# A planned kernel of attention, a state-space convolution and a gate: Toeplitz loads spaced by waits on score sets, another model of instruction supply, and a new rank for the last convolution

## The chip, the cores and the metric

The kernel runs on one core of one Trainium2 chip. The metric is the device time of one execution in microseconds (us); the median of several runs is compared. The engines of the core run side by side, each with its own queue of instructions, executed in order: TensorE (PE), VectorE (DVE), ScalarE (ACT), GpSimd (POOL) and SyncE (SP). They wait for each other by semaphores. Transfers are started by SP, POOL and ACT and carried out by the core's DMA engines.

## The reference

One sequence of 2048 tokens, width 448. Three results are mixed: attention `a` with 16 query heads of width 28 and one shared key and value head, a diagonal state-space layer `b` (256 complex states per channel) computed as a long convolution, and a gate `g`.

```python
x = A_x
g = _sigmoid((x * gate_w).sum(-1, keepdims=True))
# attention: q from x @ wq (16 heads), k = x @ wk, v = x @ wv
scores = jnp.einsum("bhqd,bkd->bhqk", q, k) * (Dh ** -0.5)
p = _softmax(scores, axis=-1)
o = jnp.einsum("bhqk,bkd->bhqd", p, v)
a = o.transpose(...).reshape(B, S, H * Dh) @ wo
# state-space layer: a kernel K per channel, then a causal convolution of length 2048
P = jnp.exp(logdA[:, :, None] * l[None, None, :])
K = jnp.einsum("dn,dnl,dn->dl", Cc, P, dB).real
y = irfft(rfft(u) * rfft(K))[:L]
b = y + u * Dskip
return g * a + (1 - g) * b
```

## The kernel before

Two streams of work run side by side.

**Attention.** The scores are cut into 1024 tiles of 128 keys by 512 queries. They are taken in sets of three and two tiles by turns, 410 sets in all; a set fills three or two of five PSUM banks. For each set PE computes the scores (L1318 with four heads in row groups, L1341 with full rows; L1329 and L1332 at the end), and ACT takes one exponential over the whole set (L1373) into the tile `expT`. PE then multiplies with the values (L1392, L1386 at the end) into bank 6. Query projections (`qproj`, L873 and L882), norms and output projections (`outp`, L1133) come once per block of 64 tiles.

**Convolution.** The 448 channels are worked in 14 groups `c` of 32. For each, DVE builds tables of powers (`tables`, L954 to L1004), PE multiplies them into the kernel K (`kgen`, L1027), DVE copies it to `kstg` (L1039), and POOL writes it to the DRAM scratch `KP`. From there SP loads Toeplitz matrices (`tload`): 56 loads, each of four `dma_start` calls with 1024 rows of 1088 bytes, into three buffers in the tile `T`, from load 42 on also into two in `U`. A convolution (`conv`, 28 of them, 16 channels each) reads two loads: 128 small matmuls (L1094) into one PSUM bank, a gated copy to `cst` on DVE (L1104), 64 transposing matmuls by pieces of 16 (L1115), and an addition into the output tile `O` (L1124). `ufill` copies inputs from `T` to `U` by SP for convolutions 14 and later.

Banks 5 and 7 are shared by `conv`, `kgen`, `qproj` and `outp`: an operation with a `lock` takes one of them at its first matmul, and the one with `unlock` gives it back.

**The end.** After the last exponential the last half block is normed (`scaled`, L1197 to L1210) and projected (`last`, L1231); L1237 adds what is in `O`. One store goes out from ACT's queue and the others from SP's.

**The order.** The order on every engine is fixed before the program runs, by a planner (`Prog.schedule`). It walks through time with an estimated cost for each operation, and at each step takes the operation that can start first, ties broken by the rank `pr` (a lower one goes first). `self.waits` then turns the dependencies `o.deps` into waits on semaphores, so a dependency added while planning becomes a real wait. Terms used below:

- A load's slot is `T0` to `T4`, so `o.slot[0] == "T"` picks the Toeplitz loads.
- `block` models how PE's instructions arrive: blocks of 256 (`BLOCK`) after a first 158 (`FIRST`). When the planned PE instructions pass the end of a block, the next one is planned to be there `FETCH` (4800 ns) later, and `IDLE` (3300 ns) from 480 us on. An operation with a rank of 1 or more also leaves a reserve (`NEED`).
- `LAZY` gives operations of ranks 1.15, 1.55, 1.58 and 1.6 a margin of 200 ns after what they wait for, and 1000 ns after a Toeplitz load before 300 us (`LATE`).
- Where PE would be idle too long, the planner puts in a filler matmul (L1300).

Of the kernel before, what the change touches and what calls it, by code (L numbers as in the profile page):

```python
# [61 lines left out]
class Buf:  # L62
    def __init__(self, handle):
        self.h = handle
        self.rs = handle[:].ap[0][0]
# [26 lines left out]
class Prog:  # L92
# [4 lines left out]
    SAME = {"act": 100.0, "dve": 125.0, "pool": 150.0}  # L97
    SWITCH = 105.0
    BLOCK, FIRST, FETCH, IDLE, NEED, QUIET = 256, 158, 4800.0, 3300.0, 0.015, 480000.0
    HALF = (0.0, 0.0, 1.0)  # L100
    PORT = 0.55
    POOL = (7, 5)
    SLACK = {"pe": 500.0, "dve": 300.0}
# [5 lines left out]
    def __init__(self, nc, es):  # L109
        self.nc, self.es = nc, es  # L110
        self.ops = []
        self.lastw = {}
        self.readers = {}
        self.slots = {}
        self.commops = {}
        self.after = {}
        self.filler = None

    def op(self, eng, fn, ns, rd=(), wr=(), pr=0, lat=None, lock=None, unlock=None, comm=None, mode="f", ni=0):
        o = Op()  # L120
# [59 lines left out]
    def schedule(self):  # L180
        ops = self.ops
# [17 lines left out]
        order = {e: [] for e in ENG}  # L199
        locks = [[None, 0.0, [], b] for b in self.POOL]  # L200
        mode = None
# [3 lines left out]
        npe = 0  # L205
        block = [0.0, 0.0]
        opened = False
        past = []
        self.tot = {}
        self.clock = {e: {} for e in ENG}  # L210
# [4 lines left out]
        while done < n:  # L215
            best = None
            for e in ENG:
                T = free[e]
                for i in ready[e]:
                    o = ops[i]  # L220
                    r = max(rt[i], T)
                    if o.lock is not None:
                        L = min((x for x in locks if x[0] is None), key=lambda x: x[1], default=None)
                        if L is None:
                            continue
                        r = max(r, L[1] + (300.0 if o.pr >= 2 else 0.0))
                    for k in o.comm or ():
                        if k in comm:
                            r = max(r, ops[comm[k]].end)
                    if e == "pe":  # L230
                        j = (npe + o.ni - self.FIRST - 1) // self.BLOCK + 1
                        if j < len(block):
                            r = max(r, block[j])
                            if o.pr >= 1 and block[-1] > r:
                                left = self.FIRST + (len(block) - 2) * self.BLOCK - npe - o.ni
                                r = max(r, block[-1] - left / self.NEED)
                    key = (r, o.pr, i)
                    if best is None or key < best[0]:
                        best = (key, e, i)
            assert best is not None, "scheduler stuck"  # L240
            (r, _, _), e, i = best
            o = ops[i]
            spare = [x for x in locks if x[0] is None and x[1] <= free[e]]
            if e == "pe" and (opened or spare) and r > self.FWIN and self.filler is not None and npe > self.FIRST + self.BLOCK:
                T = free[e]
                j = (npe + 2 - self.FIRST - 1) // self.BLOCK + 1
                w = self.FILL + (self.SWITCH if mode != "f" else 0.0) + (self.SWITCH if o.mode != "f" else 0.0) - 50.0
                past = [x for x in past if x[1] > T - self.FWIN]
                busy = sum(x[1] - max(x[0], T - self.FWIN) for x in past)
                if r - T >= w and busy < self.FLOW * self.FWIN and (j >= len(block) or block[j] <= T):  # L250
                    b = 6 if opened else spare[0][3]
                    o = self.op("pe", lambda x, b=b: self.filler(x, b), self.FILL, rd=["one", "id"], ni=2)
                    if not opened:
                        for d in spare[0][2]:
                            o.deps[d] = 1
                    rt.append(0.0)
                    need.append(0)
                    succ.append([])
                    n += 1
                    i, r = o.i, T  # L260
                    ready[e].append(i)
            ready[e].remove(i)
            if e == "pe" and o.mode != mode:
                r = max(r, free[e] + self.SWITCH)
                mode = o.mode
            if e == "pe":
                past.append((r, r + o.ns * o.act))
                opened = o.psb == 1 if o.psb else opened
            if e == "pool" and o.slot is None:
                for d in reversed(order[e]):  # L270
                    if ops[d].slot is None:
                        o.deps[d] = 1
                        break
            order[e].append(i)
            for k in o.comm or ():
                if k in comm:
                    o.deps[comm[k]] = 1
                comm[k] = i
            if o.lock is not None:
                L = min((x for x in locks if x[0] is None), key=lambda x: x[1])  # L280
                for d in L[2]:
                    o.deps.setdefault(d, 1)
                L[0] = o.lock
                o.lock.bank = L[3]
                L[2] = []
            nw = self.waits(e, o)
            if e == "pe":
                npe += o.ni + max(0, nw - 1)
                while npe > self.FIRST + (len(block) - 2) * self.BLOCK:
                    block.append(r + (self.FETCH if r < self.QUIET else self.IDLE))  # L290
            if o.slot is not None:
                free[e] = r + o.iss * o.ndma
                s = r if e == "pool" else max(r, dmafree)
                end = max(s + o.ns, free[e]) + self.DMA_NS + o.extra
                dmafree = max(dmafree, s) + o.ns
            else:
                ns = o.ns
                if e == "pe" and self.HALF[0] < r < self.HALF[1]:
                    ns *= self.HALF[2]
                free[e] = r + ns  # L300
                end = free[e] + o.lat
                if e == "pool" and o.ns >= 500.0:
                    free["dve"] = max(free["dve"], r) + self.PORT * o.ns
            o.end = end
            if o.unlock is not None:
                L = [x for x in locks if x[0] is o.unlock][0]
                L[0], L[1] = None, end + self.SEM_NS
                L[2].append(i)
            for j in succ[i]:
                need[j] -= 1  # L310
                x = ops[j]
                if i not in x.deps:
                    t = free[e]
                elif x.eng == e and o.slot is None and e == "pe":
                    t = free[e]
                elif x.eng == e and o.slot is None:
                    t = free[e] + self.SAME[e]
                else:
                    t = end + self.SEM_NS
                    if x.eng == "pe" and x.pr in self.LAZY:  # L320
                        t += self.LAZY[x.pr] if o.slot is None else self.LATE if o.slot[0] == "T" and r < 300000.0 else 0.0
                    if x.pr == 1.45:
                        t += self.FAR
                    elif x.pr >= 2 or x.pr == 1.5:
                        t += self.SLACK.get(x.eng, 0.0)
                rt[j] = max(rt[j], t)
                if need[j] == 0:
                    ready[x.eng].append(j)
            done += 1
# [79 lines left out]
class Kernel:  # L409
# [669 lines left out]
    def conv(self, c):  # L1079
        pg = self.pg  # L1080
        X = ("cx", c)
        cs = c % 2
        ps = px = self.grp()
        for k in range(4):
# [5 lines left out]
            for n in range(8):  # L1090
                def mm(e, k=k, n=n, to=to, gi=gi, tbuf=tbuf):
                    m0, par = 2 * (n // 2), n % 2
                    for j in range(4):
# [4 lines left out]
                    return r  # L1098
                first = k == 0 and n == 0
                o = pg.op("pe", mm, 56, mode="c", ni=8, rd=[("T", s), ("Uc", c % 14), ("Ub", 0), ("Ub", 1)] + [("Uf", c % 14, j) for j in range(7)],  # L1100
                      wr=[X] + ([("cst", cs)] if first else []), pr=1.6,
                      lock=ps if first else None)
                self.cm[c, 8 * k + n] = o.i
        pg.op("dve", lambda e: e.tensor_tensor(self.cst.v(0, P, cs * 512, [[128, 4], [64, 2], [1, 64]]),  # L1104
# [3 lines left out]
        Y = ("yx", c)  # L1108
# [9 lines left out]
                                 start=(mu == 0), stop=(mu == 1), tile_position=(0, 64 * par), skip_group_check=True)  # L1118
            return r
        for k in range(4):  # L1120
            o = pg.op("pe", lambda e, k=k: yt(e, k), 70, mode="h", ni=8, rd=[("cst", cs), "id"], wr=[Y], pr=1.55)
        self.lastC = o.i
        ov = self.O.v(0, P, 15 * D + 16 * c, [[-D, 16], [1, 16]])
        pg.op("dve", lambda e: e.tensor_tensor(ov, ov, px.v(0, P, 0, [[1, 16], [16, 16]]), ALU.add),  # L1124
# [363 lines left out]
```

## Time and profile before

| | us |
|---|---|
| median of 3 runs | 500.31 (500.03 to 502.58) |
| the profiled execution's own time | 499.53 |
| its span, first to last instruction | 497.8 |
| first exponential L1373 starts | 21.30 |
| last exponential ends | 490.73 |
| last table operation on DVE (L1004) ends | 453.52 |
| Toeplitz loads issued | 80.74 to 473.92 |

How to read it: the span is the stretch that the profile shows, and the time of the execution contains 1.73 us around it. In a row of a timeline the first number is the start, the second the length, then engine, line, operation, output and input, and how many instructions were merged into the row; in brackets stands the idle time of the engine just before it and what ended that. SPq is SP's queue of transfers: the length there is the time of issuing, not of moving data. "issue" names idle time in which the engine waited for no semaphore that the profile shows. A row of a table by stretches gives the stretch, its length, busy time of the engine and the number of instructions, the granted TensorE clock, the share of DMA and GB/s. A group's row gives the busy time, the mean of one in ns, and the idle time ahead of the group with what ended most of it.

### The profile page before, as it was taken

The numbers are of one execution on the slowest core, as the hardware profiler recorded it, in microseconds if no ns is written. First come the engines' busy times: TensorE is split into PE (matmuls) and PEld (weight loads), VectorE is DVE, ScalarE is ACT, GpSimd is POOL, SyncE is SP. The second block draws the span as 40 slices with busy tenths as digits, with TensorE's granted clock in tenths as the row PEclk, the third lists the DMA queues.
The fourth block names the chain that finished last, engine by engine and source line by source line (L and its number), as shares of the span: only waits on it lengthen the run. The fifth ranks groups of instructions, "written<-read, shape, count | busy, mean of one in ns | idle before, by whom it ended". The sixth has DMA issues, their size and how long they took to land.

```text
span 497.8 us, 17345 instructions
## 1 busy us (share of the span) xinstructions
PE 476.5 (96%) x7641; PEld 208.2 (42%) x7641; DVE 455.1 (91%) x867; ACT 484.2 (97%) x436; POOL 146.2 (29%) x282
## 2 busy tenths in 40 slices
PE   8899999999999999899999999999999999999997
PEld 6432233343443444444344344444444344344553
DVE  6999999999999999999999999998999999995313
ACT  6999999999999999999999999999999999999995
POOL 2102044234143433224306044520612524251110
PEclk9999999999999999999999999999999999999999
DMA  8997696928529556893953962689793596759742
GB/s 266 324 173 185 118 157 133 261 74 250 152 49 284 166 155 126 247 246 57 288 129 51 285 156 77 184 244 290 176 283 39 144 314 185 212 135 302 234 160 70
DMA packets 152423, 91.86 MB, mean 185 GB/s; under 512 B 84538, under 2 KB 148332, under 8 KB 152348
## 3 DMA queue, kind: packets, MB, share of 16 engines
q1 hardware_dynamic: 143370, 81.21, 61.4%
q0 software_dynamic: 8704, 9.41, 7.6%
q8 instruction: 60, 0.98, 0.8%
q10 hardware_dynamic: 274, 0.14, 0.1%
q14 instruction: 15, 0.12, 0.1%
HBM read 73.61 MB, written 5.23 MB: 158 GB/s over the span
## 4 chain that ended last, share of the span: by engine, by line
ACT 86%; PE 7%; DMA 2%; issue 0%; SPq 0%
ACT expT L1373 85%; DMA T<-KP_scratch 2%; PE psS L1341 1%; PE psS L1318 1%; PE psB L1392 1%; PE psB L1294 1%; PE psS L1231 1%; PE psX L1094 0%; PE psS L1094 0%; SPq L158 0%; PE psB L1300 0%; PE psS L1027 0%; PE psS L873 0%; PE psB L1386 0%; PE psX L1027 0%
## 5 line engine op out<-in xcount | busy, mean ns | idle before, releaser
L1373 ACT ACTIVATE expT<-psS 128x1536 bf16<-128x1536 f32 (+1 forms) x410 | 464.5, 1410 | 2.5 <-PE psS L1341 1.5
L968 DVE TENSOR_TENSOR tab<-tab,mbf 128x512 bf16<-128x512 bf16 (+4 forms) x140 | 139.7, 1002 | 0.0
L1318 PE MATMUL psS<-qT,kT 29*128 29x512 bf16 x684 | 95.7, 385 | 10.7 <-ACT expT L1373 5.5
L1392 PE MATMUL psB<-expT,vaug 128*32 128x512 bf16 x1000 | 99.9, 390 | 0.1
L1341 PE MATMUL psS<-qM,kT 128*128 128x512 bf16 x316 | 95.1, 384 | 1.2 <-ACT expT L1373 0.5
L158 POOL DMA_DIRECT2D KP_scratch<-kstg x104 | 57.4, 559 | 78.1 <-DVE kstg L1039 74.8
L983 DVE TENSOR_TENSOR tab<-tab 128x256 bf16<-128x256 bf16 (+4 forms) x140 | 77.3, 576 | 0.0
L1392 PEld LDWEIGHTS psB<-expT,vaug 128*32 128x32 bf16 x1000 | 25.6, 93 | 73.3 <-issue 70.5
L158 POOL DMA_DIRECT2D qM<-qT x64 | 32.4, 514 | 62.9 <-DVE qT L885 33.0
L1318 PEld LDWEIGHTS psS<-qT,kT 29*128 29x128 bf16 x684 | 23.7, 91 | 64.3 <-ACT expT L1373 51.8
L1300 PE MATMUL psB<-ident,one 128*128 128x512 bf16 x148 | 48.2, 384 | 0.0
L158 POOL DMA_DIRECT2D rdenB<-R_scratch x60 | 31.0, 523 | 48.8 <-DMA R_scratch<-denT 48.7
L1094 PE MATMUL psX<-T,U 128*26 128x128 bf16 (+3 forms) x1728 | 38.6, 221 | 1.2 <-issue 1.0
L1094 PE MATMUL psS<-T,U 128*26 128x128 bf16 (+3 forms) x1536 | 35.6, 221 | 1.1 <-DMA T<-KP_scratch 1.1
L1094 PEld LDWEIGHTS psX<-T,U 128*26 128x26 bf16 (+3 forms) x1728 | 29.6, 105 | 15.0 <-issue 10.0
L158 POOL DMA_DIRECT2D denT<-acc x15 | 10.7, 711 | 85.6 <-DVE acc L1153 72.6
L1094 PEld LDWEIGHTS psS<-T,U 128*26 128x26 bf16 (+3 forms) x1536 | 27.3, 105 | 13.3 <-issue 7.6
L997 DVE TENSOR_TENSOR tab<-tab,tmp 128x1984 bf16<-128x1984 bf16 x28 | 32.4, 1184 | 0.0
L1341 PEld LDWEIGHTS psS<-qM,kT 128*128 128x128 bf16 x316 | 19.0, 97 | 28.5 <-ACT expT L1373 19.5
L991 DVE TENSOR_TENSOR tmp<-tmp,mq 128x64 bf16<-128x64 bf16 (+4 forms) x70 | 25.4, 363 | 0.0
L914 DVE TENSOR_TENSOR msq<-seedz 128x512 f32<-128x512 f32 (+1 forms) x40 | 24.7, 618 | 0.0
L1300 PEld LDWEIGHTS psB<-ident,one 128*128 128x128 bf16 x148 | 13.3, 97 | 22.1 <-issue 14.4
(186 smaller groups left out, 491.2 us busy)
## 6 DMA issues: line engine op xcount, KB each, us to landing
T<-KP_scratch SPq DMA_DIRECT2D x204, 272.0 KB, 4.9
U<-KP_scratch SPq DMA_DIRECT2D x20, 272.0 KB, 5.5
rdenB<-R_scratch POOLq DMA_DIRECT2D x60, 64.0 KB, 4.1
U<-cst SPq DMA_DIRECT2D x1, 3584.0 KB, 25.0
qM<-qT POOLq DMA_DIRECT2D x64, 32.0 KB, 3.3
tab<-in_A_x_dram SPq DMA_DIRECT2D x4, 448.0 KB, 4.7
O<-in_A_x_dram SPq DMA_DIRECT2D x16, 112.0 KB, 4.8
O<-cst SPq DMA_DIRECT2D x1, 1792.0 KB, 9.6
```

The lines of the kernel that those rows point to most:

```text
L158: return [e.dma_start(o, i, **kw) for o, i in pairs]
L914: pg.op("dve", lambda e: e.tensor_tensor(m2(msq), z2, z2, ALU.mult), el(2 * n), rd=[kr, ki] + first, wr=["msq"], pr=pr)
L968: mul = lambda e, o, a, b: e.tensor_tensor(o, a, b, ALU.mult)
L983: vo(lambda e, dv=dv, tv=tv, k=k: e.tensor_tensor(dv, dv, tv, ALU.add if k else ALU.subtract), n, [kt[k], kd[k]], [kd[k]], 1.92 if lv else ...
L991: vo(lambda e, w=w, lv=lv: e.tensor_tensor(rho.v(0, P, (32 - 2 * w) * 2, [[64, 32], [2, w], [1, 2]]), rho.v(0, P, (32 - w) * 2, [[64, 32], ...
L997: vo(lambda e, k=k: e.tensor_tensor(tab.v(0, P, FM + k * FP + 2, [[64, 32], [2, 31], [1, 2]]), tab.v(0, P, lm + k * PL + 62, [[64, 32], [- ...
L1094: r = e.matmul(ps.v(32 * j, 32 - m0, 128 * k, [[1, 128]]), self.U.v(0, P, (4 * gi + j) % UA // 2 * 128 + 2 * (2 * m0 + par) + j % 2, [[4, ...
L1300: return e.matmul(t.v(0, P, off, [[1, 512]]), self.one.v(0, P, 2, [[0, P]]), self.ident.v(0, P, 0, [[0, 4], [1, P]]), start=b != 6, stop=b ...
L1318: r = e.matmul(self.psS.v(0, P, 512 * b, [[1, 512]]), kT.v(32 * h, DH + 1, 128 * kt, [[1, 128]]), qT.v(32 * h, DH + 1, 512 * (i % 2), [[1, ...
L1341: return e.matmul(self.psS.v(0, P, 512 * b, [[1, 512]]), kT.v(0, P, 128 * kt, [[1, 128]]), self.qM.v(0, P, (i % 2) * XQ + 512 * h, [[1, 51 ...
L1373: o = pg.op("act", lambda e: e.activation(expT.v(0, P, 512 * es[0], spread(es, n)), self.psS.v(0, P, 512 * bs[0], spread(bs, n)), AF.Exp, ...
L1392: r = e.matmul(self.psB.v(32 * h, 32, 0, [[1, 512]]), vaug.v(0, P, 32 * kt, [[1, 32]]), expT.v(0, P, 512 * ring[t], [[1, 512]]), start=(kt ...
```

## The change

Three things are altered in the planner and in two ranks; no operation of the computation is added or taken away.

```diff
     BLOCK, FIRST, FETCH, IDLE, NEED, QUIET = 256, 158, 4800.0, 3300.0, 0.015, 480000.0
+    LOAD, BEHIND, ALONE, BEGUN = 2600.0, 3700.0, 700.0, 300.0
+    OPEN = (80000.0, 440000.0)
+    GAP, SPACED = 6500.0, (80000.0, 440000.0)
...
+        self.moving = []
...
+        lastT = 0.0
...
+                    if o.slot is not None and o.slot[0] == "T" and self.SPACED[0] < r < self.SPACED[1]:
+                        r = max(r, lastT + self.GAP)
                     key = (r, o.pr, i)
...
+            if o.slot is not None and o.slot[0] == "T":
+                if self.SPACED[0] < r < self.SPACED[1]:
+                    for d in reversed(order["act"]):
+                        if ops[d].end <= r:
+                            o.deps[d] = 1
+                            break
+                lastT = r
...
                 while npe > self.FIRST + (len(block) - 2) * self.BLOCK:
-                    block.append(r + (self.FETCH if r < self.QUIET else self.IDLE))
+                    behind = max((z - r for b, z in self.moving if b < r - self.BEGUN), default=0.0)
+                    block.append(r + (self.LOAD + min(max(behind, self.ALONE), self.BEHIND) if self.OPEN[0] < r < self.OPEN[1]
+                                      else self.FETCH if r < self.QUIET else self.IDLE))
...
+                if o.ns > 1000.0 and e == "sp":
+                    self.moving = [x for x in self.moving if x[1] > r - 20000.0] + [(r, end)]
...
-                      wr=[X] + ([("cst", cs)] if first else []), pr=1.6,
+                      wr=[X] + ([("cst", cs)] if first else []), pr=1.6 if c < 27 else 0.85,
...
-            o = pg.op("pe", lambda e, k=k: yt(e, k), 70, mode="h", ni=8, rd=[("cst", cs), "id"], wr=[Y], pr=1.55)
+            o = pg.op("pe", lambda e, k=k: yt(e, k), 70, mode="h", ni=8, rd=[("cst", cs), "id"], wr=[Y], pr=1.55 if c < 27 else 0.8)
```

Between 80 and 440 us of planned time a Toeplitz load is planned no sooner than 6.5 us after the one before, and it gets a wait for the last operation on ACT that the plan has ended by then, which is mostly the exponential of a score set. In the same stretch a block of PE instructions is planned to arrive 3300 ns after the one before when nothing is moving, and up to 6300 ns when a transfer of SP (a Toeplitz load or the larger of the U copies) began at least 300 ns earlier and is still under way, by what is left of it. The matmuls of convolution 27 get the rank 0.85 instead of 1.6 and its transposes 0.8 instead of 1.55; with that they no longer fall under `LAZY` and leave no reserve of instructions.

## The prediction

> **What bounds the kernel now.** I read the page's shares first, then its chain of waits, then the timelines of the two places where that chain leaves ScalarE.
>
> ```profile
> PE 476.5 (96%) x7641; PEld 208.2 (42%) x7641; DVE 455.1 (91%) x867; ACT 484.2 (97%) x436; POOL 146.2 (29%) x282
> ...
> q8 instruction: 60, 0.98, 0.8%
> ...
> ACT 86%; PE 7%; DMA 2%; issue 0%; SPq 0%
> ...
> L1373 ACT ACTIVATE expT<-psS 128x1536 bf16<-128x1536 f32 (+1 forms) x410 | 464.5, 1410 | 2.5 <-PE psS L1341 1.5
> ```
>
> ScalarE is busy for 97% of the span, and 410 exponentials (L1373) are 464.5 of its 484.2 us. The idle column gives only 2.5 us ahead of them. It understates a little, since neighbours overlap, so I took the starts from the trace: the next exponential begins 1.330 us (median) after one of three tiles and 0.903 us after one of two. What exceeds these medians sums to 6.26 us between 80 and 440 us, and that is all the change can win in the stretch it re-plans. Two places hold 2.86 us of it. First, by the timeline at 208 us:
>
> ```profile
> 208.13 0.41 PE L1094 MATMUL psX<-T,U 128*26 128x128 bf16 x15
> 209.51 0.49 PE L1094 MATMUL psX<-T,U 128*30 128x128 bf16 x21 [0.96 <-issue]
> ...
> 210.58 1.02 ACT L1373 ACTIVATE expT<-psS 128x1024 bf16<-128x1024 f32 x1 [0.56 <-PE psS L1341]
> ...
> 211.80 1.45 ACT L1373 ACTIVATE expT<-psS 128x1536 bf16<-128x1536 f32 x1 [0.20 <-PE psS L1318]
> ```
>
> PE stops for 0.96 us in a run of equal matmuls with no semaphore to wait for. Queue q8 moved 60 blocks (0.98 MB, 16 KB each); 7641 matmuls, as many weight loads and 61 waits are 15,343 instructions, so a block holds 256. In the DMA records the block asked for near 203.05 moved only at 207.03 to 208.18, when the load issued at 200.84 was ending (its data to 207.48). From 80 to 440 us, request to arrival took 1.6 to 3.2 us where no load was moving, and up to 5.8 us behind one that had just begun. The two late exponentials lost 0.90 and 0.32: 1.22 us. Second, at 339 us:
>
> ```profile
> 338.14 0.40 PE L1392 MATMUL psB<-expT,vaug 128*32 128x512 bf16 x4
> ...
> 339.60 0.25 PE L1094 MATMUL psS<-T,U 128*32 128x128 bf16 x4 [1.06 <-DMA T<-KP_scratch]
> ...
> 340.74 2.60 ACT L1373 ACTIVATE expT<-psS 128x1024 bf16<-128x1024 f32 x2 [0.75 <-PE psS L1341]
> ```
>
> A convolution matmul stands in PE's queue before its Toeplitz load has landed, and the scores behind it are late. Here 0.88 and 0.25 are lost, and at 329.2 and 336.3 us, after like waits, 0.20 and 0.33: 1.64 us. The other 3.40 us are some twenty pieces of 0.05 to 0.27 us, behind long runs of convolution, table or projection matmuls between two score sets.
>
> SyncE's queue, by its timeline, shows how the loads come:
>
> ```profile
> 196.24 16.36 SPq L158 DMA_DIRECT2D T<-KP_scratch  x16
> 213.16 0.71 SPq L158 DMA_DIRECT2D U<-T  x1
> 214.28 5.16 SPq L158 DMA_DIRECT2D T<-KP_scratch  x4
> 219.48 15.90 SPq L158 DMA_DIRECT2D U<-T  x7
> 235.43 4.83 SPq L158 DMA_DIRECT2D T<-KP_scratch  x6
> ```
>
> Four issues are one load: five loads within 23 us, then 16 us of none. Between 80 and 440 us, 31 of 47 gaps between load starts are under 6.5 us, the least 2.6; alone, a load's data move for 3.1 to 4.6 us.
>
> VectorE is the second bound:
>
> ```profile
> 80.00:440.00 360.00, 355.57 (x663) 1.00 0.67 181
> ```
>
> It idles 4.43 us in 360 (busy 355.57), 1.14 and 1.28 of that in the same two stalls.
>
> **The change, part by part.** *Spacing of loads.* Enforcing 6.5 us on the trace's starts pushes a load by 4.6 us on average, by 12.9 at most; every group but one is caught up before the next comes. A block request then meets at most one load, and a load no other's data, so its landing is what the plan assumes. I take 1.4 of the 1.64 us as gained: the 0.20 at 329.2 came from a landing only 0.26 us late, without a margin of its own past 300 us. Bounds: 0 and 1.64.
>
> *The wait itself.* It adds no instruction to ScalarE. SyncE stands on the score set; behind it are later loads, the U copies and the early stores. A U copy is first needed by convolution 14 (it starts at 281.43 in the trace), while the copies begin at 185.2, so tens of us of cover exist. Without it a late copy would cost what the late loads cost, 0.2 to 1.1 us each. Price: 0.
>
> *The supply model.* A block was planned 4.8 us after the one before; now 3.3 with nothing moving and up to 6.3 behind a load. Both lie above what the trace shows for their case (3.2, 5.8), so the 1.22 us should go; I take 1.2, bounds 0 and 1.22.
>
> [...]
>
> *What the new plan costs.* 3.3 instead of 4.8 lets PE's runs be 1.45 times as dense between loads, and loads moved by 4.6 us of a table cycle of 29.4 us (kgen's last copies, L1039, at 77.3 and 459.0, over 13 cycles) put 16% of the convolution work into stretches that now hold other work. No row shows such a plan. From the 3.40 us of small pieces: 16% is 0.5, 45% is 1.5; I take 0.9, toward the lower, since the loads' bursts are also thinned. Bounds: all small pieces gone (3.4 gained), or doubled (3.4 lost).
>
> *Convolution 27.* Its 128 matmuls and 4 groups of transposes pass the output projections (rank 0.9) in PE's queue, lose the 0.2 us margin after a load, and ignore the reserve on instruction blocks. Its two loads keep their rank, and the stores that its sum releases (SyncE, 488.26) end before ScalarE issues the last one at 495.57, so they gain nothing. The rows at the end:
>
> ```profile
> 485.57 0.69 DVE L1104 TENSOR_TENSOR cst<-psS,omq 128x512 bf16<-128x512 f32 x1 [4.90 <-PE psS L1094]
> ...
> 487.81 0.42 DVE L1124 TENSOR_TENSOR O<-O,psS 128x256 bf16<-128x256 bf16 x1 [0.68 <-PE psS L1115]
> ...
> 492.19 0.35 PE L1237 MATMUL psS<-O,ident 128*128 128x448 bf16 x1
> ...
> 495.00 0.54 ACT L1254 ACTIVATE O<-psS 128x448 bf16<-128x448 f32 x1 [1.89 <-PE psS L1231]
> ```
>
> The last row is also the end of the chain of waits. Convolution 27 ends VectorE's 4.90 us wait at 485.57; its sum is done at 488.23, and PE reads O again at 492.19. Earlier by 2 to 3 us, it frees PE from other work before 490.73, where the last exponential ends. The 7.07 us after that are the last half's own path, with at most 0.4 us of queueing: onT ends at 493.98, the last projection starts at 494.61. I take 0.2; bounds 0.4 gained to 0.3 lost, if a block of instructions (one is crossed at 490.78) moves into this path.
>
> *Sum:* -1.2 - 1.4 + 0.9 - 0.2 = -1.9 us. Bounds: -1.22 - 1.64 - 3.4 - 0.4 = -6.7 and 3.4 + 0.3 = +3.7. The profiled execution took 499.53 (span 497.8 and 1.73 around it), so it becomes 497.6. The median of the runs is 0.78 above it, at 500.31 (500.03 to 502.58), and becomes **498.4**. A difference of 0.5%, 2.5 us, is about what can be told here from no change.
>
> **Rivals.** *The stalls move.* The order of some 15,000 instructions is made anew; one new stall of the size seen (1.22, or 1.13 from the set at 340) and small pieces at their upper estimate (1.5) leave -1.2 - 1.4 + 1.5 + 1.1 - 0.2 = -0.2: 500.1. For it: ScalarE has no more than two score sets of cover, so any PE stop of 1 us shows. The wait ties SyncE to a score set and not to a time, so a load that is late for another reason still pushes its successor. Against: the places that set off the two stalls are what the new model describes. Chance 0.25, of which 0.04 is that a block's delay doesn't depend on loads at all. That mechanism would keep the 1.22: -1.4 + 0.9 - 0.2 = -0.7, 499.6. The block that waited from 203.05 to 207.03 speaks against it. [...]
>
> *Thinner all round.* Spread loads break up the long convolution runs and the small pieces halve: -1.2 - 1.6 - 1.7 + 0.5 = -4.0, 496.3, where 0.5 is what remains of new lateness. For it: convolutions follow landings in groups now. Against: it needs all parts to pay. Chance 0.17.
>
> *Slower: PSUM held longer.* A convolution takes one of two banks (5 and 7) from its first matmul to its last sum, 12.0 us on average, and needs two loads. With starts 6.5 apart instead of about 3.3 it holds 3.2 us more: 30.4 instead of 24.0 of each cycle's 58.7 bank-us. Table matmuls (kgen), query projections and output projections use the same two; a late kgen holds up VectorE's next tables, and VectorE has no slack to 440 us. At the end there are 3.96 us of cover, 488.23 to 492.19, so it decides from 0.28 us per cycle (3.96/14). At 0.5 us per cycle VectorE ends 7.0 later: 7.0 - 4.0 = +3.0, 503.3. For it: 355.57 of 360 busy. Against: 28 bank-us per cycle are left for the others, and query projections have a 29 us period. Chance 0.20.
>
> **How the numbers follow.** The forecast itself has 0.38, with its own range 497.2 to 499.8. The range 496.0 to 502.6 takes in the second and third cases and part of the fourth. Faster by over 0.5% (under 497.8): 0.17 and about a third of 0.38, 0.30. Slower (over 502.8): 0.20. Within: 0.50.
>
> **What would show it.** The 0.96 us stop on "issue" and the 1.06 us wait for T are gone, exponentials' idle time is under 2.5 us, no two load starts between 80 and 440 us are under 6 us apart, VectorE's wait ahead of the last L1104 is under 4 us. If "issue" stops of half a microsecond appear between loads, 3.3 was too little; if VectorE idles clearly over 4.43 us before 440 us with kgen's copies (L1039) waiting, the slower rival is right. An idle gain at unchanged time would mean that the exponentials themselves became slower.

## The result, and the profile after

The changed kernel takes 503.06 us (median of 20 runs, 500.51 to 505.75) against 500.29 for the one before (20 runs, 498.74 to 505.63): a ratio of 1.0049, interval 1.003 to 1.0068. (Ratios here and below compare fast runs alone and are not the ratio of the two medians.) It became slower by 2.8 us where 1.9 of gain were forecast, and lies above the forecast's range of 496.0 to 502.6. By each run's mean granted clock (one stretch of 3.4 us at half the clock, as the profile of after shows two, takes 3.4 * 0.5/500 = 0.003 off it), 16 of the 20 runs of after had one or two such stretches and 25 of 106 of the kernel before had any; the runs of the kernel before with one are about 2.6 us longer (medians 502.4 and 499.8), and the 4 of after without one have a median of 501.4. The profiled execution of after took 504.81 (span 503.1), 1.75 above the median, and has two of these stretches (0.993), so its losses are larger than those of a typical run. Rows of its page:

```profile
PE 464.9 (92%) x7555; PEld 209.1 (42%) x7639; DVE 455.6 (91%) x867; ACT 484.5 (96%) x436; POOL 145.3 (29%) x282
...
ACT 71%; DVE 12%; PE 11%; DMA 3%; SPq 2%; issue 1%; POOL 0%
...
L1391 ACT ACTIVATE expT<-psS 128x1536 bf16<-128x1536 f32 (+1 forms) x410 | 464.7, 1403 | 6.7 <-PE psS L1336 4.2
```

This trace has 7555 matmuls beside 7639 weight loads (7641 of each before): 84 records of matmuls are missing, so PE's busy time is understated here, and weight loads are the better count. The exponentials themselves cost what they did (464.7 us against 464.5); their idle time rose from 2.5 to 6.7, and ScalarE's share of the chain of waits fell from 86 to 71%. Counted as in the prediction (starts beyond 1.330 and 0.903 us after the one before), lateness from 80 to 440 us hardly moved, 6.26 before and 6.40 after. Past 440 us, which the change does not re-plan, it rose from 0.65 to 4.77, and the tail after the last exponential grew from 7.06 to 7.79. Of the profiled execution's 5.3 us of loss, 4.1 and 0.7 lie there.

**Inside the stretch.** Both stalls shown of before are gone: at 208 us PE runs without a stop, and no 1.06 us wait stands at 339. A new place took over, by the timeline at 234 us:

```profile
233.89 0.48 PE L1112 MATMUL psX<-T,U 128*32 128x128 bf16 x20 [1.06 <-DMA T<-KP_scratch]
...
234.74 1.45 ACT L1391 ACTIVATE expT<-psS 128x1536 bf16<-128x1536 f32 x1 [0.79 <-PE psS L1336]
...
236.00 0.63 PE L1359 MATMUL psS<-qM,kT 128*128 128x512 bf16 x1 [0.33 <-issue]
...
236.68 1.02 ACT L1391 ACTIVATE expT<-psS 128x1024 bf16<-128x1024 f32 x1 [0.49 <-PE psS L1359]
...
238.39 1.45 ACT L1391 ACTIVATE expT<-psS 128x1536 bf16<-128x1536 f32 x1 [0.69 <-PE psS L1336]
```

A convolution waits 1.06 us for load 18, and three sets in a row are late, by 1.05, 0.61 and 0.81 us: 2.47 together, nearly the 2.86 that the two old stalls held. Only the first is the wait itself. The table by stretches (columns: the stretch and its length, then busy time of PE, its weight loads, DVE, ACT, POOL, then clock, DMA share, GB/s) has the rest:

```profile
232.00:235.20 3.20, 2.14 (x58) 1.25 (x60) 3.20 (x10) 2.41 (x3) 1.42 (x3) 0.93 0.67 119
235.20:238.40 3.20, 2.87 (x53) 1.27 (x43) 3.20 (x9) 2.02 (x3) 0.00 (x0) 0.53 1.01 293
238.40:242.00 3.60, 3.50 (x21) 1.10 (x20) 3.60 (x8) 3.60 (x4) 0.57 (x1) 1.00 0.72 158
```

After the wait the granted TensorE clock is about half, 0.53 in this row: the record of the clock has 0.5 from 234.78 us on for 3.41 us. One 512-column matmul, 0.38 to 0.39 us elsewhere, lasts 0.63 there.

**Past 440 us.** Before, ScalarE's row there is one unbroken run of 46 exponentials; after, it is broken:

```profile
438.84 51.89 ACT L1373 ACTIVATE expT<-psS 128x1536 bf16<-128x1536 f32 x46
```

```profile
439.38 16.08 ACT L1391 ACTIVATE expT<-psS 128x1536 bf16<-128x1536 f32 x14
456.20 22.74 ACT L1391 ACTIVATE expT<-psS 128x1536 bf16<-128x1536 f32 x20 [0.75 <-PE psS L1336]
480.70 1.45 ACT L1391 ACTIVATE expT<-psS 128x1536 bf16<-128x1536 f32 x1 [1.76 <-PE psS L1336]
482.74 1.02 ACT L1391 ACTIVATE expT<-psS 128x1024 bf16<-128x1024 f32 x1 [0.59 <-PE psS L1359]
484.25 11.02 ACT L1391 ACTIVATE expT<-psS 128x1536 bf16<-128x1536 f32 x10 [0.49 <-PE psS L1347]
```

PE's rows of after at the two breaks name what stopped the scores:

```profile
455.52 0.32 PE L1133 MATMUL psS<-ident,cst 128*64 128x60 bf16 x7 [1.00 <-issue]
...
479.64 0.70 PE L1112 MATMUL psX<-T,U 128*26 128x128 bf16 x36 [2.00 <-issue]
```

These are stops in runs of equal matmuls with no semaphore to wait for, the kind that stood at 208 us before. By the planner's count a block is asked for when PE has issued 158 + 256 j instructions (weight loads, matmuls and waits). The trace has no record of the request, so this moment is an estimate; in the profiles of before and after each of the 60 records on queue q8 begins behind one such point, 0.6 us at the soonest, and its end is the arrival. In all profiles of this case together, PE has 20 stops of over 0.6 us on "issue" after 80 us, and each lies 35 or 36 instructions behind such a point. At the one of before and the two of after, PE goes on 1.24 to 1.57 us after a block's arrival (at 208.18, 453.95 and 478.40). So they are taken here for stops at the border of a block. The block asked for at 470.76 arrived at 478.40, 7.6 us later; the blocks asked for at 448.14 and 453.78 took 5.8 and 7.2, and before, blocks behind loads in this stretch took 3.4 to 5.3. SyncE's queue after shows what they stood behind:

```profile
438.74 2.55 SPq L162 DMA_DIRECT2D T<-KP_scratch  x4
...
443.38 5.69 SPq L162 DMA_DIRECT2D T<-KP_scratch  x8
449.12 5.96 SPq L162 DMA_DIRECT2D U<-KP_scratch  x8
...
466.23 8.18 SPq L162 DMA_DIRECT2D T<-KP_scratch  x12
474.45 2.64 SPq L162 DMA_DIRECT2D U<-KP_scratch  x4
```

The last eight loads come back to back in both kernels, 2.6 to 3.9 us apart within each group of four (before they start at 440.19 to 450.52 and at 462.18 to 470.49): the spacing ends at 440 us. What differs is the work that meets them. Counting weight loads, as many matmuls, and waits, PE has 2542 instructions left at 440 us after and 2399 before. Of the 143 more, 72 convolution matmuls with their weight loads make 144, and the rest cancels. Before's stretch there, by the table by stretches, had PE busy for 48.26 of 50 us and ScalarE without a gap (columns: PE, weight loads, DVE, ACT, POOL, clock, DMA share, GB/s):

```profile
440.00:490.00 50.00, 48.26 (x1164) 25.09 (x1160) 22.17 (x34) 50.00 (x46) 7.78 (x15) 1.00 0.68 208
```

### The profile page after: what moved, and what is told of

It reads as the page before. It is cut to its first block, busy times and chain, and to the rows that moved or that the text cites. A ratio compares the mean times of both kernels' runs of the same rounds, so it can differ in the third digit from the quotient of the medians.

```text
span 503.1 us, 17277 instructions
## 1 busy us (share of the span) xinstructions
PE 464.9 (92%) x7555; PEld 209.1 (42%) x7639; DVE 455.6 (91%) x867; ACT 484.5 (96%) x436; POOL 145.3 (29%) x282
## 4 chain that ended last, share of the span: by engine, by line
ACT 71%; DVE 12%; PE 11%; DMA 3%; SPq 2%; issue 1%; POOL 0%
ACT expT L1391 71%; DVE tab L986 3%; DVE tab L1001 2%; PE psS L1359 2%; DMA qM<-qT 2%; SPq L162 2%; PE psB L1410 1%; PE psS L1336 1%; DMA T<-KP_scratch 1%; PE psX L1112 1%; DVE tab L1015 1%; PE psS L656 1%; PE psB L1318 1%; DVE tmp L1009 1%; PE psS L1249 1%
## 5 line engine op out<-in xcount | busy, mean ns | idle before, releaser
L1391 ACT ACTIVATE expT<-psS 128x1536 bf16<-128x1536 f32 (+1 forms) x410 | 464.7, 1403 | 6.7 <-PE psS L1336 4.2
L1359 PE MATMUL psS<-qM,kT 128*128 128x512 bf16 x243 | 79.2, 384 | 12.6 <-issue 8.8
L1112 PE MATMUL psX<-T,U 128*26 128x128 bf16 (+3 forms) x1728 | 40.2, 225 | 3.1 <-issue 2.0
L1112 PEld LDWEIGHTS psX<-T,U 128*26 128x26 bf16 (+3 forms) x1728 | 30.8, 107 | 18.9 <-issue 13.0
L1015 DVE TENSOR_TENSOR tab<-tab,tmp 128x1984 bf16<-128x1984 bf16 x28 | 32.2, 1182 | 0.1
L1318 PEld LDWEIGHTS psB<-ident,one 128*128 128x128 bf16 x145 | 12.9, 97 | 21.7 <-issue 14.9
```

The costliest lines, as they stand in the source:

```text
L1015: vo(lambda e, k=k: e.tensor_tensor(tab.v(0, P, FM + k * FP + 2, [[64, 32], [2, 31], [1, 2]]), tab.v(0, P, lm + k * PL + 62, [[64, 32], [- ...
L1112: r = e.matmul(ps.v(32 * j, 32 - m0, 128 * k, [[1, 128]]), self.U.v(0, P, (4 * gi + j) % UA // 2 * 128 + 2 * (2 * m0 + par) + j % 2, [[4, ...
L1318: return e.matmul(t.v(0, P, off, [[1, 512]]), self.one.v(0, P, 2, [[0, P]]), self.ident.v(0, P, 0, [[0, 4], [1, P]]), start=b != 6, stop=b ...
L1359: return e.matmul(self.psS.v(0, P, 512 * b, [[1, 512]]), kT.v(0, P, 128 * kt, [[1, 128]]), self.qM.v(0, P, (i % 2) * XQ + 512 * h, [[1, 51 ...
L1391: o = pg.op("act", lambda e: e.activation(expT.v(0, P, 512 * es[0], spread(es, n)), self.psS.v(0, P, 512 * bs[0], spread(bs, n)), AF.Exp, ...
```

## The experiments

Three theories were set against each other. A: the change pushes convolution work past 440 us, where loads come back to back and blocks are planned at a flat time, and the loss is made there. B: any new order has new stalls, wherever they fall. C: the prediction's slow rival, PSUM banks held longer.

**One part at a time.** Each of the first three keeps one part of the change and puts the others back.

```diff
-    OPEN = (80000.0, 440000.0)
+    OPEN = (0.0, 0.0)
...
-                      wr=[X] + ([("cst", cs)] if first else []), pr=1.6 if c < 27 else 0.85,
+                      wr=[X] + ([("cst", cs)] if first else []), pr=1.6,
...
-            o = pg.op("pe", lambda e, k=k: yt(e, k), 70, mode="h", ni=8, rd=[("cst", cs), "id"], wr=[Y], pr=1.55 if c < 27 else 0.8)
+            o = pg.op("pe", lambda e, k=k: yt(e, k), 70, mode="h", ni=8, rd=[("cst", cs), "id"], wr=[Y], pr=1.55)
```

> Only the spacing of the loads and its waits; supply model and last rank as before. Theory A (work pushed past 440 us meets an end in which loads come back to back and blocks of instructions are planned at a flat 4.8 us): slower than before by most of the change's loss, ratio 1.003 to 1.008, with stops on issue of 1 to 2 us after 440 us. Theory B (any new order has one or two stalls of its own, wherever they fall): anything from 0.997 to 1.008, stalls not tied to the end. Theory C (convolutions hold PSUM longer, VectorE late): ratio as in A, but VectorE's idle time before 440 us over 8 us, against 4.4 before the change.

Measured: 503.88 against 500.26, 1.0082 (1.0053 to 1.0111). 2545 instructions were left at 440 us.

```diff
-    GAP, SPACED = 6500.0, (80000.0, 440000.0)
+    GAP, SPACED = 6500.0, (0.0, 0.0)
...
-                      wr=[X] + ([("cst", cs)] if first else []), pr=1.6 if c < 27 else 0.85,
+                      wr=[X] + ([("cst", cs)] if first else []), pr=1.6,
...
-            o = pg.op("pe", lambda e, k=k: yt(e, k), 70, mode="h", ni=8, rd=[("cst", cs), "id"], wr=[Y], pr=1.55 if c < 27 else 0.8)
+            o = pg.op("pe", lambda e, k=k: yt(e, k), 70, mode="h", ni=8, rd=[("cst", cs), "id"], wr=[Y], pr=1.55)
```

> Only the supply model between 80 and 440 us; no spacing, rank as before. Theory A: the stop near 208 us is gone and nothing is pushed past 440, so 1.2 us faster to equal: ratio 0.996 to 1.001. Theory B: anything from 0.997 to 1.008. Theory C: not slower, ratio 0.997 to 1.001.

Measured: 504.31, 1.0088 (1.0057 to 1.0119); 2490 instructions left.

```diff
-    OPEN = (80000.0, 440000.0)
+    OPEN = (0.0, 0.0)
...
-    GAP, SPACED = 6500.0, (80000.0, 440000.0)
+    GAP, SPACED = 6500.0, (0.0, 0.0)
```

> Only the two ranks of convolution 27. All theories: the order differs only in the last 25 us or so; ratio 0.998 to 1.002. If the ranks alone cost more than 1 us, a part of the loss is that the last convolution takes PE's time from the last score sets.

Measured: 500.30, 1.0001 (0.9979 to 1.0023). Each of the first two parts alone costs over 0.8%, more than the whole change (the intervals overlap), and the rank alone nothing. In the profiles of the first two the lateness of 80 to 440 us is 6.53 and 6.07, near the 6.26 of before, so B's stalls do not add up there; VectorE idles 4.75 and 4.43 us in that stretch, where C asked for more than 8. Past 440 the lateness is 2.02 and 2.40, and the tail 9.99 and 9.98 instead of 7.06.

A, too, was right only in part. It had the time of the first run, but not its stops of 1 to 2 us: past 440 us PE's longest stop on "issue" there is 0.5 us, and most of the loss is the tail. It missed the second (0.996 to 1.001 expected), since the supply model alone also leaves work behind at 440 us. And the third profile, in which PE's order is that of before up to 478 us, has a block that took 7.0 us (asked for at 450.95) and a stop of 1.10 us at 452.94 us, where before's profile has none: one profile does not tell how often an order stops.

**Is it the transfers at the end?** The changed kernel in its own order, with the last eight loads cut to a fraction of their bytes:

```diff
-            to = bass.AP(tensor=buf.h, offset=h * rs + o, ap=[[4 * rs, 32], [TC, 8], [1, TC]])
+            n = TC if gi < 48 else 32
+            to = bass.AP(tensor=buf.h, offset=h * rs + o, ap=[[4 * rs, 32], [TC, 8], [1, n]])
-            lst.append((to, dram(self.KP, h * 512 + 1 + 8 * gi * KW, [[1, 32], [KW, 8], [1, TC]])))
+            lst.append((to, dram(self.KP, h * 512 + 1 + 8 * gi * KW, [[1, 32], [KW, 8], [1, n]])))
```

> The changed kernel in the same order, with loads 48 to 55 moving 32 of each row's 544 elements; the rest of these rows keeps older data, so part of the convolution of the last channels is left out. Theory A: blocks asked for after 440 us come within 3 us, the stops of 1.0 and 2.0 us on issue are gone, the last exponential ends near 491, ratio 0.997 to 1.001. Theory B agrees if its stalls are supply stalls. Theory C: PSUM and order are unchanged, so the loss stays, ratio 1.003 to 1.007.

Measured: 499.93 against 500.26, 0.999 (0.9964 to 1.0017). ScalarE's timeline from 440 us on is whole again:

```profile
439.61 51.82 ACT L1392 ACTIVATE expT<-psS 128x1536 bf16<-128x1536 f32 x46
```

Blocks asked for past 440 us took 1.7 to 3.8 us there. The table by stretches, the changed kernel first, this one second (columns as above):

```profile
440.00:490.00 50.00, 44.15 (x1095) 23.50 (x1103) 21.50 (x32) 46.41 (x41) 9.18 (x17) 0.97 0.74 227
```

```profile
440.00:490.00 50.00, 48.11 (x1192) 25.46 (x1195) 22.63 (x35) 50.00 (x45) 8.89 (x18) 1.00 0.30 60
```

In the same order PE issues 1195 weight loads in the 50 us instead of 1103. So PE can do the larger backlog in time, and what went with the bytes of the loads are the stops on "issue". Whether the thinner loads land sooner themselves was not shown; the stops that went were not on T. How much is lost beside full loads depends on where the blocks and stops fall: e1_spacing_only and g1_spacing_supply_capped, whose orders leave as much work, issue 1172 and 1182 weight loads in these 50 us with the same 227 GB/s moving and at full clock. The same thin loads in the kernel before are the control:

> The control for the thinned loads: the kernel before in its own order, loads 48 to 55 moving 32 of 544 elements (a part of the last channels' convolution is left out). Theory A: before has no backlog and only 0.65 us of lateness after 440 us, so little to regain: 0.997 to 1.000. If thinning speeds up any order by what the changed kernel regained: 0.993 to 0.996, and the thinned runs prove nothing about the backlog.

Measured: 500.47 against 499.79, 1.0004 (0.998 to 1.0029). The thin loads are worth nothing where the backlog is 682 matmuls (as counted just below) and the whole loss where it is 752.

**Is it the backlog?** The kernel before, where only convolution 22 may not begin before score set 370 (it began at 437.3 us). Measured by what the planned order leaves after the 960th value matmul, 713 matmuls of all kinds are then left, against 682 before and 752 in the change. In the traces 436, 404 and 476 of those left are matmuls of convolutions, which is the whole difference:

```diff
+            if s == HOLDSET:
+                self.holdset = o.i
...
+        pg.after[self.cm[22, 0]] = self.holdset
```

> The kernel before, with one thing altered: convolution 22 may not begin before score set 370 (near 445 us; in the kernel before it begins at 437.5). Up to there the order is the one of before, after it about 50 more matmuls are left than before, as in the changed kernel. Theory A (backlog at the end, where blocks of instructions wait behind back-to-back loads): slower by about the change's loss or more, since the last rank is as before: ratio 1.003 to 1.010, stops on issue after 450 us, and convolution 27 ends 5 to 10 us later than 485.5. Theory B (stalls fall where they like): 0.998 to 1.003. Theory C (PSUM held longer, VectorE late before 440 us): no change, 0.999 to 1.002.

Measured: 502.36 against 500.18, 1.0029 (1.0003 to 1.0055). This is just under A's range and inside B's, and convolution 27 ends 4.0 us later than before, not 5 to 10, so time alone does not decide between the two. The same marks as in the change appear in its profile, PE first, then ScalarE:

```profile
478.26 0.86 PE L1095 MATMUL psX<-T,U 128*28 128x128 bf16 x48 [0.80 <-issue]
```

```profile
439.24 39.66 ACT L1376 ACTIVATE expT<-psS 128x1024 bf16<-128x1024 f32 x35
479.50 4.63 ACT L1376 ACTIVATE expT<-psS 128x1536 bf16<-128x1536 f32 x4 [0.60 <-PE psS L1319]
484.67 8.72 ACT L1376 ACTIVATE expT<-psS 128x1536 bf16<-128x1536 f32 x8 [0.54 <-PE psS L1330]
```

With the thin loads on top:

> As the run with convolution 22 held, in the same order, and loads 48 to 55 move 32 of each row's 544 elements (a part of the last channels' convolution is left out). Theory A: the blocks come within 3 us, the loss is gone, ratio 0.997 to 1.001. If instead the late convolutions themselves are the cost, whatever the blocks do, the loss stays: 1.003 to 1.010.

Measured: 501.03, 1.0002 (0.998 to 1.0024). None of the change's three parts is in these kernels. Holding back one convolution makes a small loss, and with thin loads none can be told. The two intervals overlap, so that the loss goes with the transfers rests here on the profiles: lateness past 440 us is 2.13 us with full loads and 0.59 with thin ones, 0.65 before. The loss is smaller than the change's; how much of the rest is the larger backlog, the place at 234 us and the clock was not separated.

**The rank in company.** The change without it:

```diff
-                      wr=[X] + ([("cst", cs)] if first else []), pr=1.6 if c < 27 else 0.85,
+                      wr=[X] + ([("cst", cs)] if first else []), pr=1.6,
...
-            o = pg.op("pe", lambda e, k=k: yt(e, k), 70, mode="h", ni=8, rd=[("cst", cs), "id"], wr=[Y], pr=1.55 if c < 27 else 0.8)
+            o = pg.op("pe", lambda e, k=k: yt(e, k), 70, mode="h", ni=8, rd=[("cst", cs), "id"], wr=[Y], pr=1.55)
```

> The changed kernel with convolution 27 ranked as before. Theory A: the rank is what saves the end in the changed kernel, whose stretch after the last exponential was 7.8 us against 10.0 in the two runs of one part alone: ratio 1.007 to 1.012, and that stretch is 9.5 to 10.5 us. If the rank does nothing: 1.004 to 1.006.

Measured: 504.68 against 500.18, 1.0095 (1.0063 to 1.0127), beside 1.0049 (1.003 to 1.0068) with it. Its timeline of ScalarE at the end:

```profile
483.22 8.72 ACT L1391 ACTIVATE expT<-psS 128x1536 bf16<-128x1536 f32 x8 [1.15 <-PE psS L1347]
497.22 0.98 ACT L1272 ACTIVATE O<-psS 128x448 bf16<-128x448 f32 x2 [5.28 <-PE psS L1255]
```

The last exponential ends at 491.94, earlier than in the changed kernel's profile (495.27), but ScalarE's copy of the last projection waits 5.28 us, as convolution 27 comes behind the last exponentials (its sum ends at 496.8) and the tail is 9.99 us. With the rank it is pulled in front of them: a shorter tail, bought with scores that come later. Not all of that difference is the rank's: PE's order is the changed kernel's up to 485 us, yet this profile has only one stop on "issue" of over 0.6 us past 440 us, at 482.89, and lateness of 2.54 us there instead of 4.77. So the stops of one order differ from execution to execution.

**Which numbers make the backlog.** The change without spacing:

```diff
-    GAP, SPACED = 6500.0, (80000.0, 440000.0)
+    GAP, SPACED = 6500.0, (0.0, 0.0)
```

> The changed kernel without the spacing: supply model up to 6.3 us and the last rank. In order of instructions it has 1178 matmuls left after the 912th value matmul and 754 after the 960th, against 1144 and 682 before and 1238 and 752 in the changed kernel. Theory A: the loss is there without any spacing, because the model's 6.3 us alone pushes work past 440: ratio 1.003 to 1.007, the stretch after the last exponential about 7.8 us thanks to the rank. If only spacing makes the changed kernel slow: 0.997 to 1.001.

Measured: 503.33 against 500.28, 1.0063 (1.0034 to 1.0091). Then the same with the upper end of the supply model at 2600 + 2200 ns, 4.8 instead of 6.3 us, run twice:

```diff
-    LOAD, BEHIND, ALONE, BEGUN = 2600.0, 3700.0, 700.0, 300.0
+    LOAD, BEHIND, ALONE, BEGUN = 2600.0, 2200.0, 700.0, 300.0
```

> Supply model with its upper end lowered from 6.3 to 4.8 us (BEHIND 2200), so that it never plans a block later than before; rank as in the change; no spacing. The number of matmuls left after 440 us is then that of before. Theory A: no loss, ratio 0.997 to 1.002. Theory B: 0.997 to 1.008. If a faster supply between loads is what costs (PE's runs too dense), 1.004 or more.

Measured: 499.73 against 500.18, 0.9984 (0.9966 to 1.0002).

> The version with capped supply, the last rank and no spacing once more, since its first interval (0.9966 to 1.0002) ends at no change. If it is faster than before: again under 0.999. If it is the same: 0.999 to 1.001.

Measured: 499.73 against 499.79, 0.9996 (0.9977 to 1.0016). With 4.8 the plan has before's backlog of 682 matmuls: without spacing it is the 6.3 that makes the plan slow, and the 3.3 alone brings no gain that can be told. Spacing with the cap:

> Spacing and rank as in the changed kernel, supply model capped at 4.8 us. Left after the 960th value matmul: 754 (changed kernel 752, before 682). Theory A: the spacing alone makes the backlog, so the loss stays: 1.003 to 1.007. If the model's 6.3 us is the only cause: 0.998 to 1.001.

Measured: 501.90 against 499.79, 1.0033 (1.0014 to 1.0053), 754 matmuls left: spacing makes the backlog without the 6.3 too. Two further sizes, the gap in the change

```diff
-    GAP, SPACED = 6500.0, (80000.0, 440000.0)
+    GAP, SPACED = 6600.0, (80000.0, 440000.0)
```

> The changed kernel with 6.6 us between loads in place of 6.5: a new order with the same backlog (1237 matmuls left after the 912th value matmul, 753 after the 960th). Theory A: 1.003 to 1.008, like the changed kernel. Theory B: unrelated to it, 0.997 to 1.010, with stalls before 440 us in other places.

and the flat time of the capped kernel

```diff
-    BLOCK, FIRST, FETCH, IDLE, NEED, QUIET = 256, 158, 4800.0, 3300.0, 0.015, 480000.0
+    BLOCK, FIRST, FETCH, IDLE, NEED, QUIET = 256, 158, 4000.0, 3300.0, 0.015, 480000.0
```

> The version with the supply model capped at 4.8 us, the last rank and no spacing, with a block planned 4.0 us after the one before outside 80 to 440 us, so that the end is planned denser: 493 matmuls left after the 972nd value matmul (527 before). Theory A: less backlog, ratio 0.995 to 1.000, unless blocks that really take 3.4 to 5.3 us in the end make PE stop: then 1.000 to 1.004.

Measured: 502.12 against 500.28, 1.0047 (1.0016 to 1.0077), with 753 left and a 2.2 us stop on "issue" past 440; and 500.47, 1.0014 (0.9994 to 1.0034), with 682 left. That is not the gain that A had for less backlog; its longest stop on "issue" past 440 us is 0.6 us.

Taken together, with full loads: the four orders with before's 404 convolution matmuls left at that point (rank only, capped twice, capped with 4.0 us) have ratios of 0.9984 to 1.0014; the one with 436 has 1.0029; the seven with 476 (the change, spacing only, supply only, no spacing, no rank, spacing with the cap, gap of 6.6) have 1.0033 to 1.0095. So whether there is a loss goes with the backlog; how large it is does not follow from the backlog alone. Last, both windows of the change carried on to 490 us:

```diff
-    OPEN = (80000.0, 440000.0)
+    OPEN = (80000.0, 490000.0)
...
-    GAP, SPACED = 6500.0, (80000.0, 440000.0)
+    GAP, SPACED = 6500.0, (80000.0, 490000.0)
```

> The changed kernel with both stretches (spacing and supply model) extended from 440 to 490 us. It describes the end better, and has 805 matmuls left after the 960th value matmul (752 in the changed kernel, 682 before) and 248 after the 1044th (41 and 23). Theory A: more backlog is more loss, ratio over 1.010, although stops on issue after 440 become rarer. If the loss came from a bad model of the end, so from stops alone: 0.998 to 1.003.

Measured: 508.62 against 500.28, 1.0172 (1.0144 to 1.0199). SyncE's queue and ScalarE's end:

```profile
472.31 16.90 SPq L162 DMA_DIRECT2D T<-KP_scratch  x12
490.75 3.07 SPq L162 DMA_DIRECT2D U<-KP_scratch  x4
```

```profile
482.01 8.72 ACT L1391 ACTIVATE expT<-psS 128x1536 bf16<-128x1536 f32 x8 [0.69 <-PE psS L1347]
503.14 0.54 ACT L1272 ACTIVATE O<-psS 128x448 bf16<-128x448 f32 x1 [12.42 <-PE psS L1255]
```

Here the stops on "issue" past 440 us shrink to 0.4 us and the last exponential ends at 490.73, as before. The spacing does what it is for, but the last load goes out at 490.75, where it was 474.45 in the changed kernel and 470.49 before, and everything that hangs on it comes after the exponentials. Spacing the last loads shrinks the stops and makes the end late; leaving them dense lets stops of 1 to 2 us happen while much work meets them. No kernel tried is faster than the one before by more than the noise.

## Why the prediction was wrong, point by point

**The bound** held: the loss is lateness of exponentials and the path after them. But the prediction took "all the change can win in the stretch it re-plans" as the place where it could also lose. The size of its frame, 80 to 440 us, was the mistake: lateness there changed by 0.14 us, past it by 4.12.

**The failed step is "What the new plan costs"**, with the clause "every group but one is caught up before the next comes". It priced denser runs and moved loads by the small pieces of lateness inside the stretch: 0.9 us, with 3.4 as a bound. The runs showed work pushed over 440 us instead, 4.12 us of lateness there and 0.73 of tail in the profile. The pushes were also larger than worked out: the loads of 80 to 440 us began 7.8 us later on average and 18.7 at most (4.6 and 12.9 expected), load 47 at 438.74 instead of 425.33. Even by the prediction's own way of enforcing 6.5 us, load 47 moves by 10.1 us, and no time is left to catch up before the window ends. Load 48 comes only 3.2 us later; the work in between is not caught up. PE's convolution matmuls (first to last weight load) show the delay grow:

| convolution | before, us | after, us |
|---|---|---|
| 22 | 437.31 to 442.13 | 441.37 to 445.93 |
| 24 | 448.96 to 462.65 | 453.80 to 466.04 |
| 26 | 470.29 to 476.48 | 473.93 to 482.84 |
| 27 | 478.56 to 485.23 | 485.24 to 494.17 |

A lag of 4 us at 440 is 9 us for the last one. An estimate of the size from before's own rows was open to the prediction, had it asked what work crosses the end of the window: 1160 weight loads and as many matmuls ran from 440 to 490 us, 46 instructions per us, so 143 more need 143/46 = 3.1 us if that stretch has nothing to spare. That this comes near the 2.8 measured is in part luck: 1.6 of the 2.8 show in the runs at full clock, the stretch had something to spare (1172 to 1195 weight loads in other runs), and orders with the same backlog lose from 0.33 to 0.95%.

**Spacing of loads**, 1.4 us gained: the wait at 339 us went, but the wait at 234 us came, of the same 1.06 us, in the stretch that the spacing governs. The other spaced kernels e1_spacing_only, e4_thin_last_loads and g1_spacing_supply_capped have it too (1.14, 1.01 and 0.98 us), while the profile of e6_no_rank, with the same order there, has 0.43 us of it and 0.88 us at 338.71: the places of these waits shift between executions as well. "Its landing is what the plan assumes" was wrong there: load 18 was issued at 225.22 and its data moved from 226.61 to 233.27, 6.7 us, where 3.1 to 4.6 was the time alone. U copies issued at 218.54 and 227.83 lie around it; that they are the cause was not tested.

**The wait itself**, 0: nothing showed against it. Five of the gaps between load starts fell under 6 us (5.44 to 5.86) and none to the 2.6 of before, so the waits hold the spacing nearly as planned.

**The supply model**, 1.2 us gained: the stop at 208 us is gone in the changed kernel, but the runs do not put that down to this part. With the spacing alone it is gone too. With the model and no spacing a new stop on "issue" stands inside the window, 1.05 us at 178.31 (e2_supply_only) and 1.80 us at 179.03 (e5_no_spacing). With the model capped at 4.8 us the old one is back (0.95 and 1.12 us). The prediction argued that both its ends "lie above what the trace shows" and saw only safety in that. A planned delay above the real one is also a cost, since work goes out later than it could: with 4.8 instead of 6.3 and no spacing the loss disappears (1.0063 to 0.9984 and 0.9996), and the 1.2 us do not show as a clear gain in any run.

**Convolution 27**, 0.2 us: right alone (1.0001), mis-sized in company. Without it the loss is 1.0095 instead of 1.0049. The cover of 3.96 us between its sum and the next reading of O, which the prediction read off correctly, is what the backlog used up. "VectorE's wait ahead of the last L1104 is under 4 us" came true and misled: it was 0.52 us after, but only since VectorE had other work shortly before; the operand arrived at 494.55, 9 us later than before.

**The rivals.** "The stalls move" is what happened between 80 and 440 us, where the small pieces neither thinned out nor doubled. "PSUM held longer" had the right sign, which is luck: its mechanism does not show. A convolution held its bank for 12.6 us on average instead of 12.0, not for 3.2 more; VectorE's busy time in the stretch, 355.57 before, is

```profile
80.00:440.00 360.00, 355.50 (x662) 1.00 0.68 178
```

so it idles 4.50 us instead of 4.43. That a block's delay does not depend on loads at all, 0.04 of the first rival, does not fit the runs: in e4_thin_last_loads, where little moved, blocks took 1.7 to 3.8 us past 440 us and no such stop stands there; behind full loads in the changed kernel's profile they took up to 7.6 us, with a stop of 2.00 us.

## What to carry to other kernels

Where a change delays work inside a window, count what crosses the window's end and ask what the stretch that receives it can still take, instead of pricing the delay inside the window alone. A model that plans a resource to be later than it is avoids its stalls by sending work out late, which can be the same loss in another place. And a part that shows nothing alone can be worth about half a per cent beside others: here the rank only repaired a part of what the other two had done.

## What the runs showed of the hardware

**Instruction blocks behind loads.** Past 440 us a block of 16 KB takes, from the estimated request to its arrival, 1.7 to 3.8 us with thin loads (e4_thin_last_loads), and up to 7.6 us behind full ones in the changed kernel's profile; PE then stops for up to 2.00 us (2.2 with a gap of 6.6 us). A late block need not stop PE: in the profile of spacing alone one took 6.1 us there, and the longest stop on "issue" is 0.5 us. All 20 stops of over 0.6 us in these profiles lie 35 or 36 instructions behind a point of the count, so at one place of a block.

**Half the clock behind short stops.** In the changed kernel's profile the granted clock is 0.5 from 234.78 and from 480.54 us on, behind stops of 1.06 and 2.00 us that ended at 233.89 and 479.64, and this lasts 3.41 us each time. The stops of 0.96 and 1.06 us in before's profile (they ended at 209.51 and 339.60) and the one of 1.00 us in the changed kernel's (455.52) brought none: the clock there is 1.0. What sets these apart was not shown, and that the stop is the cause was not tested by itself. By the 4 runs at full clock, which are few, about 1.6 of the 2.8 us come without it; the rest goes with the more frequent half clock (16 of 20 runs, against 25 of 106).
